# Fused sharp attention and softplus MLP: softplus halves split back to back, next chunk's scales made one quarter earlier

## Chip, cores and metric

The kernel runs on one core of a Trainium2 chip. The metric is device time in microseconds of one execution, inputs and output in device memory. A profile of one execution is at hand; its engines are PE (matmul; PEld is its weight load), DVE (VectorE), ACT (ScalarE), POOL (GpSimd) and SP, which issues DMAs.

## Reference

Attention keeps only scores within `tau` of the row's maximum, and its output goes through a two-layer MLP with softplus.

```python
scores = scale * q @ k.T                       # 8 batches, 8 heads, 576 rows, head size 64
thresh = max(scores, -1) - tau                 # tau = 0.02
scores = where(scores >= thresh, scores, -1e9)
attn = exp(scores - max); attn = attn / (sum(attn) + 1e-9)
x = (attn @ v) -> [4608, 512]                  # heads side by side
h = x @ w_in                                   # [4608, 2048]
out = (max(h, 0) + log1p(exp(-|h|))) @ w_out   # [4608, 512]
```

The inputs q, k, v and w_in are drawn some six times as large as the setup functions alone would give.

## The kernel before

**Attention.** A unit is one batch and two heads: 32 units of nine tiles of 128 query rows, 288 tiles in all. For each tile PE writes the scores `s` (line 480) into one of two PSUM banks; DVE takes the negated row maximum (`negm`); ACT makes `e_all` by the exponential and then the threshold `thr`; DVE masks `e_all` in place, reading the scores again, and only then is that bank free for the scores two tiles on. POOL writes the upper 16-bit half of the masked weights into `h` (the function `weights_hi`), DVE writes the remainder beside it (`weights_lo`, the DVE rows `h<-e_all,h`), a DMA transposes both, and PE multiplies them by v (`pv`, line 591). ACT copies and DVE adds the two parts of `pv` into `xp`.

**MLP.** Tokens go through the MLP in ten chunks: eight of 512 tokens, one for each batch, and two of 256 with the last 64 rows of four batches. For a chunk, `hidden` makes 16 slices of the hidden layer (line 712), each of 12 matmuls, since x and w_in are kept as two 16-bit halves. ACT takes softplus of two slices at a time and scales them (`st`). `parts_of` then splits one slice into its two 16-bit halves on POOL: a TENSOR_SCALAR for the upper half and a TENSOR_TENSOR for the lower one, named `g` in the profile. `project` multiplies by w_out (line 776); a quarter is four slices, and its results are added in SBUF (`acc`) by DVE. In the last quarter of a chunk the products of slices 12 and 13 come first, and the splits of slices 14 and 15 are held in `waits` until those products of the quarter's first output tile have been written into the program; the products with slices 14 and 15 end that output tile.

**Scales.** Before a chunk, `x_scale` makes the scale of x, and `split_x` scales and splits its four columns of `xp` into `xh` and `xl` (ACT, then POOL). `h_scales` makes three small tiles of 128x4 (three DVE instructions, in the profile `c<-p_i,sx` and two `c<-c`), which the softplus needs, and `o_scales` a fourth (`c<-c,p_o`), which `acc` needs. In the chunks after the first they are made when the chunk's first `hidden` and its first `project` are written.

**Order of the work.** The attention tiles lead. For each tile the string `PAT` says in which order its steps and slices of MLP work are written. `defer(n, f)` runs `f` at the n-th `point()` from now, and there are two points in a tile. From tile `TQ` on, the classes `Queue` keep DVE, ACT and POOL in exactly the order written; PE's order and that of the DMAs are set by the scheduler. `prep` is the list of the 32 pieces of weight conversion still to be written; two tiles pass from one piece to the next, so it runs empty at about tile 62 of 288, in the first chunk.

Of the kernel before, what the change touches and what calls it, by code (L numbers as in the profile page):

```python
# [65 lines left out]
def tile_kernel(ctx: ExitStack, tc: tile.TileContext, q, k, v, tau, w_in, w_out, out):  # L66
# [108 lines left out]
    def inverse(out_, p):  # L175

        vec.tensor_scalar(out=out_.bitcast(U32), in0=p.bitcast(U32), scalar1=EXP, scalar2=None, op0=ALU.bitwise_xor)

    def halves(hi, lo, x):
        pool.tensor_scalar(out=hi, in0=x, scalar1=1.0, scalar2=1.0, op0=ALU.mult, op1=ALU.mult)  # L180
        pool.tensor_tensor(out=lo, in0=x, in1=hi, op=ALU.subtract)
# [70 lines left out]
    def need(*key):  # L252

        while key not in ready:
            if prep and not later:
                _, f, a = prep.pop(0)
                f(*a)
            else:
                force()
# [384 lines left out]
    def load_x(u, cc):  # L644

        if u.main:
            return
        for b in range(QB):
            need("q", NPAIR * (QB * u.b + b) + cc)
        st = fpool.tile([P, QB * SR], F32, tag="xst", name=f"xst_{u.n}_{cc}")  # L650
        u.st[cc] = st
        nc.sync.dma_start(st, x_d[u.b][:, cc, :])

    def x_scale(u):
        n = NPAIR * (1 if u.main else QB)
        for i in range(n):
            need("v", n * u.b + i)

        u.sx, u.px = [cpool.tile([P, 1], F32, tag=f"sx{i}", bufs=2, name=f"sx{i}_{u.n}") for i in range(2)]
        u.ch, u.g_top, u.sg, u.co = [cpool.tile([P, NFC // 4], F32, tag=f"c{i}", bufs=2, name=f"c{i}_{u.n}")  # L660
                                     for i in range(4)]
        vec.tensor_reduce(u.sx, v_scale[:, n * u.b:n * (u.b + 1)], axis=AX.X, op=ALU.min)
        inverse(u.px, u.sx)

    def h_scales(u, g):

        if g in u.scaled:
            return
        c = slice(g, g + 1) if u.n == 0 else slice(0, NFC // 4)
        u.scaled |= set(range(c.start, c.stop))  # L670
        vec.tensor_scalar(out=u.ch[:, c], in0=p_w["i"][:, c], scalar1=u.px, scalar2=0.25, op0=ALU.mult, op1=ALU.mult)
        vec.tensor_scalar(out=u.g_top[:, c], in0=u.ch[:, c], scalar1=2.0 ** 26, scalar2=2.0 ** -13,
                          op0=ALU.mult, op1=ALU.max)
        inverse(u.sg[:, c], u.g_top[:, c])

    def o_scales(u, g):

        if g in u.unscaled:
            return
        c = slice(g, g + 1) if u.n == 0 else slice(0, NFC // 4)  # L680
        u.unscaled |= set(range(c.start, c.stop))
        vec.scalar_tensor_tensor(out=u.co[:, c], in0=u.g_top[:, c], scalar=0.25, in1=p_w["o"][:, c],
                                 op0=ALU.mult, op1=ALU.mult)

    def split_x(u, cc, n=0):
        per = 2 * TC // u.T
        if cc % per == 0:
            for l, tag in ((u.h, "xh"), (u.l, "xl")):
                t = fpool.tile([P, 2 * TC], F16, tag=tag, name=f"{tag}_{u.n}_{cc}")
                l += [t[:, i * u.T:(i + 1) * u.T] for i in range(per)]  # L690
        if u.main:
            need("x", NPAIR * u.b + cc)
            st = units[NPAIR * u.b + cc].xp[:, 0:SM]
        else:
            st = u.st.pop(cc)
        act.activation(st, st, AF.Copy, scale=u.sx)
        defer(n, lambda: halves(u.h[cc], u.l[cc], st))
# [23 lines left out]
    def softplus(u, full):  # L721


        ts, last_ = [], None
        with tc.high_priority(SPP):
            for fc, bank in reversed(full):
                t = fpool.tile([P, TC], F32, tag="st", bufs=NST, name=f"st_{u.n}_{fc}")
                i = act.activation(t, bank, AF.Softplus, scale=u.ch[:, fc // 4:fc // 4 + 1]).ins
                if last_ is not None:
                    tc.add_manual_dep(i, last_.name, mybir.DependencyInfo(  # L730
                        mybir.DependencyClass.NoSync, mybir.DependencyReason.DATA), reason="one table load")
                last_ = i
                ts.append((fc, t))
            for fc, t in reversed(ts):
                act.activation(t, t, AF.Copy, scale=u.sg[:, fc // 4:fc // 4 + 1])
        def parts():
            if u.n in waits:
                waits[u.n].append(parts)
                return
            for n, (fc, t) in enumerate(reversed(ts)):  # L740
                defer(n, lambda fc=fc, t=t: parts_of(u, fc, t))
        defer(HD[1], parts)

    waits = {}
# [2 lines left out]
    def parts_of(u, fc, t):  # L747

        home, tags, bufs = (fpool, ("gh", "gl"), NG)
        if u.tail:  # L750
            spare = [("kT", "kT", 2), ("qT0", "qT1", 1), ("nat", "nat", 2), ("vt", "vt", 2)]
            i = later_g[0] % (NG + len(spare))
            later_g[0] += 1
            if i >= NG:
                *tags, bufs = spare[i - NG]
                home = apool
        gh, gl = [home.tile([P, TC], F16, tag=tags[i], bufs=bufs, name=f"g{i}_{u.n}_{fc}") for i in range(2)]
        halves(gh, gl, t)
        for i in range(TC // u.T):
            c = slice(i * u.T, (i + 1) * u.T)  # L760
            u.g[fc + i] = (gh[:, c], gl[:, c])
# [49 lines left out]
    nq = NFC // QF  # L811
# [3 lines left out]
    def order():  # L815
        out_, at_ = [], 0
        for u in chunks:
            both = u.tail and u.n + 1 < len(chunks)
            for qt in range(nq):
                end = NFC * (u.n + (2 if both and qt == nq - 1 else 1))  # L820
                to = min(end, NFC * u.n + QF * (qt + 1) + (LT if u.tail else LS if u.T < TC else NG - QF))
                first_ = [("h", i // NFC, i % NFC) for i in range(at_, to)]
                at_ = max(at_, to)
                if qt == nq - 1 and not u.tail and u.T == TC:


                    last_o = out_.pop()[:4]
                    early.add(last_o[1:])
                    out_ += [("w", u.n), *first_, (*last_o, 0)]
                else:  # L830
                    out_ += first_

                x = u.n + 1 < len(chunks) and qt == nq - (2 if u.tail else 1)
                from_ = 1 if ("o", u.n, nq - 2, u.T // P - 1)[1:] in early and not u.tail else 0
                out_ += [("o", u.n, qt, tb, from_ + tb if x else -1) for tb in range(u.T // P)]
        return out_

    def stream():
        for cc in range(len(X0), NCC):
            split_x(chunks[0], cc)  # L840
        for it in order():
            u = chunks[it[1]]
            if it[0] == "h":
                yield from hidden(u, it[2])
                continue
            if it[0] == "w":
                waits[u.n] = []
                continue
            if it[4] >= 0:

                nx = chunks[u.n + 1]
                per = NCC * P // u.T
                for cc in range(max(0, (it[4] - 1) * per), min(NCC, it[4] * per)):
                    split_x(nx, cc)
                    if cc + 2 < NCC:
                        load_x(nx, cc + 2)
                if it[4] == 0:
                    x_scale(nx)
                    load_x(nx, 0)
                    load_x(nx, 1)  # L860
            yield from project(u, it[2], it[3])
            if it[4] >= 0 and it[3] == u.T // P - 1 and (u.n, it[2], it[3]) not in early:
                for cc in range(it[4] * per, NCC):
                    split_x(nx, cc)
# [6 lines left out]
    def defer(n, f):  # L871
        if n == 0:
            f()
        else:
            later.append((now["p"] + n, f))
# [8 lines left out]
    def force():  # L884
        _, f = later.pop(0)
        f()
# [8 lines left out]
    for n, (main, b, from_) in enumerate(spans):  # L895
        u = Chunk()
# [4 lines left out]
        u.tail = from_ >= NS  # L901
        chunks.append(u)
    ffn = stream()

    def target(g):
# [7 lines left out]
    prep = []  # L913
    for kind, g in WL:
        for m in range(4):
            n = len(prep)
# [167 lines left out]
```

## Time and profile before

| | |
|---|---|
| median of 3 runs | 1319.87 us (1319.84 to 1323.7) |
| the profiled execution | 1319.59 us, of which the instructions span 1317.8 us |
| busy, share of the span | PE 95%, DVE 71%, POOL 70%, ACT 69% |
| granted PE clock, mean | 0.994 |

The profile's page gives for each engine its busy time, for groups of instructions the count, the busy time and the idle time of the engine just ahead of them, and names what ended that idle time. A row of the timeline gives the start and length of one piece of work, and in brackets how long its engine had been idle and what released it. Matmuls overlap, so a PE with no idle time may still lose some time between two starts.

### The profile page before, as it was taken

The numbers are of one execution on the slowest core, as the hardware profiler recorded it, in microseconds if no ns is written. First come the engines' busy times: TensorE is split into PE (matmuls) and PEld (weight loads), VectorE is DVE, ScalarE is ACT, GpSimd is POOL, SyncE is SP. The second block draws the span as 40 slices with busy tenths as digits, with TensorE's granted clock in tenths as the row PEclk, the third lists the DMA queues.
The fourth block names the chain that finished last, engine by engine and source line by source line (L and its number), as shares of the span: only waits on it lengthen the run. The fifth ranks groups of instructions, "written<-read, shape, count | busy, mean of one in ns | idle before, by whom it ended". The sixth has DMA issues, their size and how long they took to land.

```text
span 1317.8 us, 21688 instructions
## 1 busy us (share of the span) xinstructions
PE 1245.7 (95%) x7153; PEld 752.0 (57%) x7153; DVE 936.2 (71%) x1738; ACT 907.2 (69%) x1715; POOL 920.2 (70%) x987
## 2 busy tenths in 40 slices
PE   5988988899999999998999899999999999999998
PEld 4655544455566566665666566655656755554455
DVE  5878888988878787888787877886677666640011
ACT  5877887886877677776777697768675867643321
POOL 2577788888777777778877786787666787564333
PEclk9999999999999999999999999999999999999999
DMA  4544458867876678787877787776667665530010
GB/s 127 159 139 126 125 129 165 180 112 149 160 149 146 139 161 152 150 148 161 149 143 145 161 149 142 145 150 132 130 125 163 115 132 114 98 78 17 1 40 17
DMA packets 395521, 168.79 MB, mean 128 GB/s; under 512 B 350448, under 2 KB 376464, under 8 KB 395408
## 3 DMA queue, kind: packets, MB, share of 16 engines
q1 hardware_dynamic: 395408, 167.40, 61.6%
q8 instruction: 57, 0.93, 0.3%
q14 instruction: 56, 0.46, 0.1%
HBM read 56.62 MB, written 10.63 MB: 51 GB/s over the span
## 4 chain that ended last, share of the span: by engine, by line
PE 57%; ACT 15%; POOL 12%; DVE 8%; issue 6%; DMA 2%; SPq 0%; POOLq 0%; ACTq 0%; DVEq 0%
PE o L776 20%; PE h L712 17%; PE s L480 9%; PE pv L591 6%; ACT L156 4%; ACT st L156 4%; POOL g L156 2%; ACT e_all L156 2%; DVE negm L156 2%; PE pv L550 2%; DVE e_all L156 2%; POOL xl L156 2%; PE tr L420 2%; POOL h L156 1%; POOL w_i L156 1%
## 5 line engine op out<-in xcount | busy, mean ns | idle before, releaser
L776 PE MATMUL o<-w_o,g 128*128 128x512 f16 x1728 | 407.9, 382 | 13.9 <-POOL g L156 11.0
L712 PE MATMUL h<-xh,w_i 128*128 128x512 f16 (+1 forms) x1280 | 360.7, 358 | 3.6 <-ACT kT L156 1.9
L156 POOL TENSOR_SCALAR h<-e_all 128x576 f16<-128x576 f32 x243 | 239.3, 985 | 121.5 <-DVE e_all L156 114.9
L156 ACT ACTIVATE e_all<-s,negm 128x576 f32<-128x576 f32 x288 | 213.8, 742 | 132.3 <-DVE negm L156 129.8
L712 PEld LDWEIGHTS <-w_i 128*128 128x128 f16 x1920 | 179.4, 98 | 165.9 <-issue 7.4
L776 PEld LDWEIGHTS <-g 128*128 128x128 f16 x1728 | 159.1, 98 | 191.4 <-POOL g L156 16.3
L156 DVE SCALAR_TENSOR_TENSOR e_all<-s,thr,e_all 128x576 f32<-128x576 f32 x288 | 233.0, 809 | 49.3 <-ACT thr L156 48.8
L156 DVE TENSOR_REDUCE negm<-s 128x1 f32<-128x576 f32 x288 | 215.2, 747 | 73.2 <-PE s L480 72.1
L156 DVE SCALAR_TENSOR_TENSOR h<-e_all,h 128x576 f16<-128x576 f32 x243 | 237.7, 978 | 2.5 <-POOL h L156 2.5
L712 PE MATMUL h<-xl,w_i 128*128 128x512 f16 (+1 forms) x640 | 229.4, 358 | 0.5 <-POOL xl L156 0.5
L156 POOL TENSOR_SCALAR g<-st 128x512 f16<-128x512 f32 x144 | 99.5, 691 | 165.1 <-ACT st L156 156.9
L156 DVE SCALAR_TENSOR_TENSOR acc<-o,c,acc 128x512 f32<-128x512 f32 x108 | 80.2, 743 | 171.8 <-PE o L776 110.6
L156 POOL TENSOR_TENSOR g<-st,g 128x512 f16<-128x512 f32 x144 | 171.2, 1189 | 12.0
L480 PE MATMUL s<-kT,q 128*128 128x288 f32 x768 | 152.9, 328 | 16.1 <-DVE e_all L156 13.6
L156 ACT ACT_TABLE_LOAD x119 | 152.7, 1283 | 3.9 <-DVE negm L156 1.9
L591 PE MATMUL pv<-eT,vt 128*128 128x288 f16 x1080 | 153.6, 288 | 1.2 <-DVE xp L156 0.4
L156 ACT ACTIVATE st<-h,c 128x512 f32<-128x512 f32 x144 | 91.2, 684 | 76.2 <-PE h L712 75.4
L480 PEld LDWEIGHTS s<-kT,q 128*128 128x128 f32 x768 | 115.0, 192 | 49.1 <-DVE e_all L156 35.6
L591 PEld LDWEIGHTS <-vt 128*128 128x128 f16 x1080 | 99.9, 98 | 37.9 <-issue 2.0
L480 PE MATMUL s<-kT,qT 128*128 128x288 f32 x512 | 107.3, 331 | 10.5 <-DVE e_all L156 8.7
L156 ACT COPY xp<-pv 64x288 f32<-64x288 f32 (+3 forms) x133 | 50.7, 385 | 87.1 <-PE pv L591 82.9
L156 ACT ACTIVATE st<-st,c 128x512 f32<-128x512 f32 x144 | 96.3, 716 | 2.3
(113 smaller groups left out, 1512.7 us busy)
## 6 DMA issues: line engine op xcount, KB each, us to landing
q<-q SPq DMA_DIRECT2D x62, 192.0 KB
kn<-in_k_dram SPq DMA_DIRECT2D x32, 256.0 KB
qn<-in_q_dram SPq DMA_DIRECT2D x32, 256.0 KB
vn<-in_v_dram SPq DMA_DIRECT2D x32, 256.0 KB
wc_i<-in_moe_w_in_dram SPq DMA_DIRECT2D x16, 512.0 KB
wc_o<-in_moe_w_out_dram SPq DMA_DIRECT2D x16, 512.0 KB
qT<-qT SPq DMA_DIRECT2D x62, 128.0 KB
out_dram<-acc SPq DMA_DIRECT2D x14, 512.0 KB
```

The costliest lines, as they stand in the source:

```text
L156: i = getattr(self.eng, name)(*args, **kwargs)
L420: nc.tensor.transpose(pr[:, c * P:(c + 1) * P], src, identr)
L480: nc.tensor.matmul(sp[:, hf, 0:HS], lhs, s.kT[j][:, hf * HS:(hf + 1) * HS], start=(m == 0), stop=(m == len(parts) - 1))
L550: nc.tensor.matmul(o[0:D, 0:n], s.vn[k_, 5 * j + c, :], h[k_, c, 0:n], start=(c == 0), stop=(c == NC))
L591: nc.tensor.matmul(o[:, 0:HS], s.vt[:, 5 * j + c, :], s.eT[j][:, c + i, x0:x0 + HS], start=(c == 0 and i == 0), stop=(c == NC and i > 0))
L712: nc.tensor.matmul(bank[:, i * u.T:(i + 1) * u.T], wi[g, cc][:, a, e], x[cc], start=(cc == 0 and m == 0), stop=(cc == NCC - 1 and m == 2))
L776: nc.tensor.matmul(o, u.g[fc][m // 2][:, sl], wo[fc][:, m % 2, :], start=(n == 0), stop=(n == 3 * QF - 1))
```

## The change

Two places of the program are touched. In `softplus`, the two slices of a pair were split at one point and the next. While `prep` still holds weight conversions this stays; after that both are split at the same point, one behind the other. In `stream`, right behind `x_scale` for the next chunk (written ahead of the last output tile of the running chunk's third quarter, and in the chunks of 256 tokens and the last ones at the start of a late quarter), the four small scale instructions for the next chunk are written at once; `need` makes sure that the scales of all weight blocks exist there. The later calls of `h_scales` and `o_scales` then find them made.

```diff
             for n, (fc, t) in enumerate(reversed(ts)):
-                defer(n, lambda fc=fc, t=t: parts_of(u, fc, t))
+                defer(n if prep else 0, lambda fc=fc, t=t: parts_of(u, fc, t))
         defer(HD[1], parts)
...
                 if it[4] == 0:
                     x_scale(nx)
+                    need("i", nq - 1)
+                    need("o", nq - 1)
+                    h_scales(nx, 0)
+                    o_scales(nx, 0)
                     load_x(nx, 0)
                     load_x(nx, 1)
```

On POOL, at the end of chunk 1, the pair of slices 14 and 15 (`g_1_14`, `g_1_15`) stands as follows before; `xh` and `xl` are the first columns of x for chunk 2:

```order
L156 TENSOR_SCALAR g_1_14_5206<-st_14_5173 128x512
L156 TENSOR_TENSOR g_1_14_5207<-st_14_5173,g_1_14_5206 128x512
L156 TENSOR_SCALAR h_132<-e_all 128x576
L156 TENSOR_SCALAR xh_0_5226<-xp_3783 128x512
L156 TENSOR_TENSOR xl_0_5227<-xp_3783,xh_0_5226 128x512
L156 TENSOR_SCALAR g_1_15_5233<-st_15_5171 128x512
L156 TENSOR_TENSOR g_1_15_5234<-st_15_5171,g_1_15_5233 128x512
L156 TENSOR_SCALAR h_132<-e_all 128x576
```

and in the changed kernel:

```order
L156 TENSOR_SCALAR g_1_14_5210<-st_14_5177 128x512
L156 TENSOR_TENSOR g_1_14_5211<-st_14_5177,g_1_14_5210 128x512
L156 TENSOR_SCALAR g_1_15_5214<-st_15_5175 128x512
L156 TENSOR_TENSOR g_1_15_5215<-st_15_5175,g_1_15_5214 128x512
L156 TENSOR_SCALAR h_132<-e_all 128x576
L156 TENSOR_SCALAR xh_0_5234<-xp_3787 128x512
L156 TENSOR_TENSOR xl_0_5235<-xp_3787,xh_0_5234 128x512
```

Slice 15 has moved ahead of one `h` and of the first `xh` and `xl`. Within a chunk the same happens to every pair, as on POOL for slices 4 and 5 of chunk 2, before:

```order
L156 TENSOR_SCALAR g_2_4_5768<-st_4_5747 128x512
L156 TENSOR_TENSOR g_2_4_5769<-st_4_5747,g_2_4_5768 128x512
L156 TENSOR_SCALAR h_132<-e_all 128x576
L156 TENSOR_SCALAR g_2_5_5789<-st_5_5745 128x512
L156 TENSOR_TENSOR g_2_5_5790<-st_5_5745,g_2_5_5789 128x512
L156 TENSOR_SCALAR h_132<-e_all 128x576
```

and in the changed kernel:

```order
L156 TENSOR_SCALAR g_2_4_5768<-st_4_5748 128x512
L156 TENSOR_TENSOR g_2_4_5769<-st_4_5748,g_2_4_5768 128x512
L156 TENSOR_SCALAR g_2_5_5772<-st_5_5746 128x512
L156 TENSOR_TENSOR g_2_5_5773<-st_5_5746,g_2_5_5772 128x512
L156 TENSOR_SCALAR h_132<-e_all 128x576 x2
```

The first of the two `h` now stands behind two more instructions and right in front of the second. The third place is DVE at the start of chunk 2, where the scales stood before, between the remainder of one tile's weights and the addition into `xp`:

```order
L156 SCALAR_TENSOR_TENSOR h_132<-e_all,h_132 128x576
L156 TENSOR_SCALAR c_2_5158<-p_i,sx_2_5157 128x4
L156 TENSOR_SCALAR c_2_5159<-c_2_5158 128x4
L156 TENSOR_SCALAR c_2_5160<-c_2_5159 128x4
L156 TENSOR_TENSOR xp_5415<-pv_0_5416,xp_5415 64x288
```

and where they stand in the changed kernel, on DVE in chunk 1, between the scale of x for chunk 2 and the row maximum of a tile:

```order
L156 TENSOR_SCALAR sx_2_5157<-sx_2_5156 128x1
L156 TENSOR_SCALAR c_2_5158<-p_i,sx_2_5157 128x4
L156 TENSOR_SCALAR c_2_5159<-c_2_5158 128x4
L156 TENSOR_SCALAR c_2_5160<-c_2_5159 128x4
L156 SCALAR_TENSOR_TENSOR c_2_5161<-c_2_5159,p_o 128x4
L156 TENSOR_REDUCE negm_5_5220<-s_131 128x1
```

The first three moved by some 28 rows and the fourth, which stood in chunk 2 ahead of a row maximum, by some 60. ACT's order is the same in both kernels. On PE single products change places at the ends of chunk 0 and chunk 5, and on SP a few DMAs.

## The prediction

> **What bounds the kernel now.** I read the page first (busy shares), then the stretches by stage, then PE's waits grouped by releaser, then the timeline around the longest of them.
>
> ```profile
> PE 1245.7 (95%) x7153; PEld 752.0 (57%) x7153; DVE 936.2 (71%) x1738; ACT 907.2 (69%) x1715; POOL 920.2 (70%) x987
> ...
> 595.50:733.70 138.20, 134.45 (x793) 82.39 (x794) 110.77 (x202) 100.94 (x185) 104.46 (x112) 1.00 0.77 149
> ```
>
> PE is busy for 134.45 of 138.20 us in chunk 3, at full clock, while DVE has 110.77 and POOL 104.46. So what counts is idle time of PE, and what is late for PE. PE's waits that the change can touch, of those grouped by releaser (us in total, times, longest):
>
> ```profile
> PE s L480 <- DVE e_all L156: 22.4, 27, 3.7
> PE o L776 <- POOL g L156: 11.0, 12, 1.9
> PE tr L413 <- DVE xp L156: 4.3, 6, 1.2
> ```
>
> The second is what the first edit is about, the third what the second edit is about, and the first is where both can do harm.
>
> **First edit, at the chunk's end.** POOL, then PE, in the end of chunk 1:
>
> ```profile
> 450.14 1.16 POOL L156 TENSOR_TENSOR g<-st,g 128x512 f16<-128x512 f32 x1
> 451.27 0.67 POOL L156 TENSOR_SCALAR h<-e_all 128x576 f16<-128x576 f32 x1
> 453.92 0.62 POOL L156 TENSOR_SCALAR xh<-xp 128x512 f16<-128x512 f32 x1 [1.98 <-ACT xp L156]
> 454.63 1.53 POOL L156 TENSOR_TENSOR xl<-xp,xh 128x512 f16<-128x512 f32 x1
> 456.13 0.61 POOL L156 TENSOR_SCALAR g<-st 128x512 f16<-128x512 f32 x1
> 456.83 1.15 POOL L156 TENSOR_TENSOR g<-st,g 128x512 f16<-128x512 f32 x1
> ...
> 453.20 1.69 PE L776 MATMUL o<-w_o,g 128*128 128x512 f16 x7
> 456.80 0.82 PE L776 MATMUL o<-w_o,g 128*128 128x512 f16 x3 [1.92 <-POOL g L156]
> 458.04 1.03 PE L776 MATMUL o<-w_o,g 128*128 128x512 f16 x2 [0.42 <-POOL g L156]
> ...
> 454.00 1.14 DVE L156 SCALAR_TENSOR_TENSOR h<-e_all,h 128x576 f16<-128x576 f32 x1
> 458.68 0.75 DVE L156 SCALAR_TENSOR_TENSOR acc<-o,c,acc 128x512 f32<-128x512 f32 x1 [3.04 <-PE o L776]
> ```
>
> The half of slice 14 is done at 451.30. Slice 15 then waits behind h, behind 1.98 us in which POOL is idle for x, and behind xh and xl, until 456.13. PE has used everything else by 454.89 (453.20 + 1.69) and idles 1.92 + 0.42 = 2.34 us. With slice 15 directly behind slice 14 its halves are done at about 451.30 + 0.62 + 0.08 + 1.15 = 453.1, before PE asks. The h that it pushes back ends at 453.8, still ahead of 454.00, where DVE reads it, and of xh at 453.92: POOL's idle time pays. So the whole 2.34 goes, and over all chunk ends the row's 11.0 us. What is late next: DVE waits 3.04 us there for the same PE product, so it moves forward with PE; I see no other wait within the 2.3 us. Ends for this term: 11.0, and half of it if x, scores or a bank take over.
>
> **First edit, within a chunk.** Here no PE wait on g is to be won, and h comes later by the 0.62 + 0.08 + 1.16 of one split. Slices 4 and 5 of chunk 2, POOL, DVE, PE:
>
> ```profile
> 501.39 1.16 POOL L156 TENSOR_TENSOR g<-st,g 128x512 f16<-128x512 f32 x1
> 502.52 0.67 POOL L156 TENSOR_SCALAR h<-e_all 128x576 f16<-128x576 f32 x1
> 503.86 1.16 POOL L156 TENSOR_TENSOR g<-st,g 128x512 f16<-128x512 f32 x1
> 504.98 1.18 POOL L156 TENSOR_SCALAR h<-e_all 128x576 f16<-128x576 f32 x1
> ...
> 503.63 0.82 DVE L156 SCALAR_TENSOR_TENSOR e_all<-s,thr,e_all 128x576 f32<-128x576 f32 x1 [1.80 <-ACT thr L156]
> 504.37 1.26 DVE L156 SCALAR_TENSOR_TENSOR h<-e_all,h 128x576 f16<-128x576 f32 x1
> 505.55 0.74 DVE L156 TENSOR_REDUCE negm<-s 128x1 f32<-128x576 f32 x1
> 506.22 0.80 DVE L156 SCALAR_TENSOR_TENSOR e_all<-s,thr,e_all 128x576 f32<-128x576 f32 x1
> ...
> 507.09 0.79 PE L480 MATMUL s<-kT,q 128*128 128x288 f32 x4
> ```
>
> The reader is to see two things. PE's scores start at 507.09, 0.07 us behind the end of DVE's mask at 507.02: any delay of DVE here is a delay of PE. And DVE's remainder at 504.37 takes 1.26 us, of which the first part passes until POOL's TENSOR_TENSOR ends at 505.02; POOL's next h, begun at 504.98, takes 1.18 instead of 0.67, until DVE is through. These two instructions don't run side by side; the second to come waits. In the changed order h ends at about 502.52 + 1.86 + 0.67 = 505.05, the next h is next on POOL and runs until 505.7, and DVE's remainder, which can't start before 505.1, ends at 505.7 + 0.62 = 6.3, that is 506.3 instead of 505.63. DVE and the scores behind it: 0.65 us late. If DVE got in ahead of the second h it would be some 0.2 us late.
>
> On this the Trainium skill ("SBUF — State Buffer", section on who interferes with whom) says that a VectorE instruction with two SBUF inputs and a GpSimd one that reads SBUF share a port pair as an exclusive lock, and that the order of issue decides who waits. The rows above agree (1.26 and 1.18 us). The rule speaks against this edit: by it the second h wins and the place costs the larger of my two values; without it the place would cost the smaller.
>
> Other pairs of the chunk, POOL's h between the two slices and the DVE row that reads it: slices 0 and 1, then 2 and 3, then 8 and 9:
>
> ```profile
> 485.58 0.67 POOL L156 TENSOR_SCALAR h<-e_all 128x576 f16<-128x576 f32 x1
> ...
> 487.21 1.49 DVE L156 SCALAR_TENSOR_TENSOR h<-e_all,h 128x576 f16<-128x576 f32 x1
> 488.73 0.46 DVE L156 TENSOR_TENSOR xp<-pv,xp 64x288 f32<-64x288 f32 x1
> ...
> 493.92 0.67 POOL L156 TENSOR_SCALAR h<-e_all 128x576 f16<-128x576 f32 x1
> ...
> 496.90 1.32 DVE L156 SCALAR_TENSOR_TENSOR h<-e_all,h 128x576 f16<-128x576 f32 x1
> ...
> 535.58 0.67 POOL L156 TENSOR_SCALAR h<-e_all 128x576 f16<-128x576 f32 x1
> ...
> 537.75 0.94 DVE L156 SCALAR_TENSOR_TENSOR h<-e_all,h 128x576 f16<-128x576 f32 x1
> 540.14 1.88 DVE L156 SCALAR_TENSOR_TENSOR h<-e_all,h 128x576 f16<-128x576 f32 x1
> ```
>
> For 0 and 1 h would be ready at 485.58 + 1.86 + 0.67 = 488.1 and the remainder, behind one more POOL instruction, end at 489.1 instead of 488.70; PE waits for that xp just behind, so I put 0.4. For 8 and 9 the remainder ends some 0.6 later than 538.69, but the next one (1.88 us, most of it waiting for POOL) absorbs part: 0.3, and the same for 12 and 13, which follow the same pattern one unit on. For slices 2 and 3 h would come at 493.92 + 2.53 = 496.45, and DVE asks at 496.90: nothing, and likewise for 6 and 7 and for 10 and 11, where DVE asks later still. Sum for a chunk 0.65 + 0.4 + 0.3 + 0.3 = 1.65, for the four chunks 1 to 4 about 6.6 us. Behind chunk 4 DVE has time, as this stretch of chunk 6 and what follows shows, so I cost it at nothing; the cover is DVE's 62.7 idle us there (181.40 - 118.73), and if it failed the price would be that of one more chunk, 1.65.
>
> ```profile
> 998.60:1180.00 181.40, 178.62 (x1099) 112.27 (x1100) 118.73 (x221) 123.53 (x213) 124.08 (x134) 1.00 0.59 115
> ```
>
> Ends for the term: 0, and 0.65 at all seven pairs of four chunks, 28 x 0.65 = 18.2. I stay nearer to the lower end, by the row of slices 2 and 3: three of the seven pairs cost nothing. On SP one load of q's rest rows falls behind two transposes and an output; no wait on it shows. In chunk 0 and chunk 5 PE's products with slice 15 move ahead of scores, as the scheduler now expects them earlier; they are counted in the 11.0.
>
> **Second edit.** No instruction is added; four per chunk move. The start of chunk 4, DVE and PE, then the place to which they go, at the end of chunk 1:
>
> ```profile
> 749.93 0.63 DVE L156 TENSOR_SCALAR c<-p_i,sx 128x4 f32<-128x4 f32 x1
> 750.60 0.38 DVE L156 TENSOR_SCALAR c<-c 128x4 f32<-128x4 f32 x2
> 750.88 0.44 DVE L156 TENSOR_TENSOR xp<-pv,xp 64x288 f32<-64x288 f32 x1
> ...
> 751.38 0.28 PE L413 MATMUL tr<-identr,k 128*128 128x128 f32 x1 [1.08 <-DVE xp L156]
> ...
> 447.25 0.76 DVE L156 TENSOR_REDUCE negm<-s 128x1 f32<-128x576 f32 x1 [0.60 <-PE s L480]
> 450.41 0.46 DVE L156 TENSOR_TENSOR xp<-pv,xp 64x288 f32<-64x288 f32 x1 [1.00 <-ACT xp L156]
> ```
>
> Without them xp starts 0.95 us earlier (750.88 - 749.93), and PE's 1.08 shrinks to about 0.1. Over the six waits of the group, 4.3 us, I take 4.0. At the new place they cost DVE their 0.63 + 0.38 + about 0.2, of which 0.60 is idle time before negm and the rest lies ahead of another idle time of 1.00: nothing reaches PE. If that cover fails, 0.6 at each of nine chunks, 5.4. Ends: -4.3 and +1.1.
>
> **The sum.** -11.0 + 6.6 - 4.0 = -8.4 us on the profiled 1319.59 gives 1311.2. The median of the runs, 1319.87, lies 0.28 above it: I forecast 1311.5, 0.6% faster. About 0.3%, 4 us, is what a measurement can tell from no change here.
>
> **Rivals.** (1) The delays of h cost nothing, because DVE gets in between the two h or makes it up at its next wait: 1319.9 - 15.0 = 1304.9, and some 1306 if a little stays. For it speaks that DVE is idle for 27 of 138 us in a chunk; against it 0.07 us between mask and scores. (2) The wait at the chunk's end is only replaced (by x, by scores, by a bank), half of 11.0 stays, and the delays of h come in full: 1319.9 - 5.5 - 4.0 + 6.6 = 1317. With the second edit failing too, 1321. Against it: no other engine is late within those 2.3 us. (3) Slower: the h behind two splits. Every moved pair of the chunks 1 to 4 makes DVE's mask late, by the lock above, as the worst does. At 28 x 0.65 = 18.2 the gain of 15.0 is gone (1323.1); it decides from 0.54 us a pair on. Seven pairs a chunk would have to behave like slices 4 and 5; three don't ask for h in time to notice. By the lock rule of the Trainium skill alone, at every pair, one would come to this case.
>
> **Chances.** As forecast, 1307 to 1315: 0.5. Rival 1: 0.22. Rival 2: 0.18, most of it within 0.3%. Rival 3: 0.1, mostly slower. So faster by over 0.3% 0.74, within 0.3% 0.18, slower 0.08. The range takes in most of rival 1 and most of rival 2: 1305 to 1319.
>
> **What would show it.** Right: PE's waits of o for POOL's g fall from 11.0 to under 1 us, those of tr for xp at line 413 from 4.3 to under 1; PE's waits of s for e_all or DVE's waits for POOL's h (2.5 us before) grow by a few us; chunks 1 to 4 shorten from 138.2 to about 136.6 us each, the part from 1180 on keeps its length. Wrong: the waits on g stay, or a chunk is no shorter though they went, or the gain is 15 us and h's delay appears nowhere.

## The result and the profile after

The changed kernel takes 1306.32 us (median of 4 runs, 1305.69 to 1307.61) against 1319.86 us (4 runs) of the kernel before: ratio 0.9892, 95% interval 0.9872 to 0.9912; between the medians lie 13.5 us. A second series (e5 below) gave 0.9906 (0.9891 to 0.9922). The forecast was 1311.5 us in a range of 1305 to 1319. The sign and the range held; the gain is 1.6 times the forecast 8.4 us. The profiled execution took 1307.61 us, its instructions span 1305.5 us.

The busy times on the page of the changed kernel:

```profile
PE 1238.5 (95%) x7153; PEld 750.8 (58%) x7153; DVE 930.4 (71%) x1738; ACT 906.0 (69%) x1715; POOL 913.2 (70%) x987
```

PE's work is the same, 7153 matmuls, and so are DVE's and POOL's counts. PE's waits of the changed kernel, grouped by releaser (us in total, times, longest):

```profile
PE s L480 <- DVE e_all L156: 26.6, 29, 4.1
...
PE topv L378 <- DVE xp L156: 1.5, 2, 1.0
PE pv L591 <- DVE xp L156: 1.4, 3, 0.5
```

Both waits that the edits were about have left the list: of o for POOL's g (11.0 before) and of tr at line 413 for DVE's xp (4.3 before) no row of 0.3 us or more is left. In their place stand 4.2 us more of s behind DVE's mask (22.4 before), the two small groups behind xp, and a few single waits of up to 1.0 us. So 15.3 us of waits went, and the largest of what came is 4.2.

Where in the program the time went is seen in stretches of 36 tiles, cut at the ends of DVE's masks of tiles 143, 179, 215, 251 and 287, with the tail behind them; first the kernel before, then the changed one (length, then busy time of PE, PEld, DVE, ACT, POOL with counts, PE clock, DMA share, GB/s):

```profile
571.50:709.70 138.20, 134.50 (x793) 82.41 (x792) 110.83 (x205) 100.94 (x185) 104.51 (x113) 1.00 0.78 149
709.70:847.90 138.20, 134.49 (x793) 82.34 (x792) 110.83 (x203) 100.89 (x185) 104.60 (x113) 1.00 0.76 149
847.90:1003.00 155.10, 151.13 (x874) 90.58 (x873) 112.84 (x210) 107.89 (x195) 113.16 (x123) 1.00 0.68 134
1003.00:1164.90 161.90, 159.12 (x989) 101.65 (x989) 110.67 (x204) 114.37 (x198) 113.52 (x120) 1.00 0.61 120
1164.90:1317.80 152.90, 147.80 (x792) 77.19 (x789) 23.63 (x44) 45.31 (x72) 59.44 (x70) 1.00 0.10 27
```

```profile
569.50:704.30 134.80, 133.72 (x793) 82.69 (x792) 109.61 (x204) 100.76 (x185) 102.95 (x113) 1.00 0.80 153
704.30:839.00 134.70, 133.65 (x793) 82.59 (x792) 109.56 (x204) 100.74 (x185) 102.89 (x113) 1.00 0.80 153
839.00:990.50 151.50, 150.49 (x874) 90.78 (x873) 112.76 (x216) 107.18 (x193) 111.91 (x122) 1.00 0.67 137
990.50:1152.50 162.00, 159.35 (x990) 101.36 (x989) 106.85 (x201) 115.29 (x199) 113.26 (x122) 1.00 0.63 120
1152.50:1305.50 153.00, 147.89 (x793) 77.28 (x790) 23.13 (x44) 45.25 (x72) 59.31 (x70) 1.00 0.10 28
```

A chunk in steady state is 3.4 to 3.6 us shorter, where the forecast had 1.6. The last stretch has kept its length, as forecast, and so has the one ahead of it. Two earlier ones belong to the sum: tiles 107 to 143 are 4.0 us shorter (some 0.6 us of it is a drop of PE's clock in the kernel before, see e3 and e4), and tiles 71 to 107 (the end of chunk 0 and the start of chunk 1), 138.81 us before, take 139.12: there the edits brought nothing in sum; why is told further down.

The end of chunk 1 in the changed kernel, POOL, PE and DVE (the whole is 2.0 us later here than in the kernel before: the mask of tile 107 ends at 434.78 us against 432.79):

```profile
451.38 0.62 POOL L156 TENSOR_SCALAR g<-st 128x512 f16<-128x512 f32 x1 [1.13 <-PE o L776]
452.08 1.54 POOL L156 TENSOR_TENSOR g<-st,g 128x512 f16<-128x512 f32 x1
453.59 0.61 POOL L156 TENSOR_SCALAR g<-st 128x512 f16<-128x512 f32 x1
454.29 1.16 POOL L156 TENSOR_TENSOR g<-st,g 128x512 f16<-128x512 f32 x1
455.42 0.67 POOL L156 TENSOR_SCALAR h<-e_all 128x576 f16<-128x576 f32 x1
...
455.14 2.76 PE L776 MATMUL o<-w_o,g 128*128 128x512 f16 x12
457.74 0.38 PE L378 MATMUL topv<-identr,vtop 128*128 128x128 f32 x2
...
456.12 1.15 DVE L156 SCALAR_TENSOR_TENSOR h<-e_all,h 128x576 f16<-128x576 f32 x1
```

The twelve products that ran as 7, 3 and 2 with two waits between now run in one piece of 2.76 us; slice 15's halves are done at 455.45, before PE comes to the products that read them. The h that was pushed back ends at 456.09 and DVE's remainder takes it at 456.12, with no idle time in its row. Counted from the end of slice 14's split (453.62), slice 15 is done 1.83 us and the h 2.47 us later, where the prediction had 1.85 and 2.52: that part came out as it drew it.

### The profile page after: what moved, and what is told of

The parts are those of the page before. It is cut to its first block, busy times and chain, and to the rows that moved or that the text cites. A ratio compares the mean times of both kernels' runs of the same rounds, so it can differ in the third digit from the quotient of the medians.

```text
span 1305.5 us, 21701 instructions
## 1 busy us (share of the span) xinstructions
PE 1238.5 (95%) x7153; PEld 750.8 (58%) x7153; DVE 930.4 (71%) x1738; ACT 906.0 (69%) x1715; POOL 913.2 (70%) x987
## 4 chain that ended last, share of the span: by engine, by line
PE 45%; ACT 18%; POOL 13%; DVE 12%; issue 7%; DMA 3%; SPq 1%; POOLq 0%; DVEq 0%; ACTq 0%
PE o L776 15%; PE h L712 14%; PE s L480 7%; ACT st L156 6%; ACT L156 5%; PE pv L591 5%; POOL g L156 4%; DVE e_all L156 3%; DVE negm L156 3%; ACT e_all L156 3%; DVE h L156 2%; PE pv L550 2%; POOL h L156 2%; POOL w_i L156 1%; POOL xl L156 1%
## 5 line engine op out<-in xcount | busy, mean ns | idle before, releaser
L776 PE MATMUL o<-w_o,g 128*128 128x512 f16 x1728 | 402.7, 380 | 3.1 <-DVE xp L156 1.6
L156 POOL TENSOR_SCALAR h<-e_all 128x576 f16<-128x576 f32 x243 | 228.0, 941 | 114.3 <-DVE e_all L156 108.3
L156 DVE SCALAR_TENSOR_TENSOR h<-e_all,h 128x576 f16<-128x576 f32 x243 | 235.8, 971 | 19.6 <-POOL h L156 19.2
L480 PE MATMUL s<-kT,q 128*128 128x288 f32 x768 | 153.1, 328 | 22.4 <-DVE e_all L156 18.5
```

The source lines that it names most:

```text
L156: i = getattr(self.eng, name)(*args, **kwargs)
L480: nc.tensor.matmul(sp[:, hf, 0:HS], lhs, s.kT[j][:, hf * HS:(hf + 1) * HS], start=(m == 0), stop=(m == len(parts) - 1))
L776: nc.tensor.matmul(o, u.g[fc][m // 2][:, sl], wo[fc][:, m % 2, :], start=(n == 0), stop=(n == 3 * QF - 1))
```

## The experiments

The softplus line and the scales were varied one by one. All ratios are to runs of the kernel before on the same chip. "End pair" means slices 14 and 15 of a chunk, "inner pairs" the seven others.

| run | end pair | inner pairs | scales | median us | ratio (95%) |
|---|---|---|---|---|---|
| e1_scales_only | apart | apart | early | 1315.79 | 0.9954 (0.9941 to 0.9968) |
| e3_end_pair_and_scales | apart (edit without effect) | apart | early | 1317.45 | 0.9969 (0.9957 to 0.9981) |
| e2_splits_only | together | together | late | 1313.91 | 0.9953 (0.9934 to 0.9971) |
| e4_inner_pairs_only | together (edit without effect) | together | late | 1315.61 | 0.9958 (0.9943 to 0.9973) |
| e5_after_again | together | together | early | 1307.82 | 0.9906 (0.9891 to 0.9922) |
| e6_end_pair_and_scales | together | apart | early | 1302.88 | 0.9866 (0.9851 to 0.9881) |
| e7_inner_pairs_only | apart | together | late | 1326.77 | 1.0046 (1.0033 to 1.006) |
| e8_h_first | together | one point on | early | 1305.46 | 0.9882 (0.9866 to 0.9898) |
| e9_end_pair_alone | together | apart | late | 1309.24 | 0.9917 (0.9899 to 0.9935) |
| e10_end_pair_three_scales | together | apart | early, three of four | 1300.81 | 0.9844 (0.9825 to 0.9864) |

**e1: the scales alone.** The softplus line stays as before; the four lines for the scales are in.

```diff
                     x_scale(nx)
+                    need("i", nq - 1)
+                    need("o", nq - 1)
+                    h_scales(nx, 0)
+                    o_scales(nx, 0)
```

> Only the second edit (the four small scale instructions moved one quarter ahead); pairs are split as before. Theory 'three parts' (end-of-chunk pair, pairs within a chunk, scales each have their own price, which add): the changed kernel's 13.5 us holds about 6 us of this part, since the start-to-start loss of PE at the starts of chunks 1 to 5 was 1.3, 0.3, 1.3, 1.2 and 0.8 us, and about 0.3 more goes where the fourth instruction stood: 1313 to 1315.5 us. Rival 'one part': nearly all comes from the end-of-chunk pair, and DVE only waits elsewhere instead: 1318 to 1320.

Measured 1315.79 us, about 5.7 us under the kernel before, more than the 4.0 of the prediction. The waits of tr at line 413 for xp are gone; those of o for POOL's g stay with 9.3 us in 8 waits.

**e2: the splits alone.** The softplus line of the change, without the scales.

```diff
-                defer(n, lambda fc=fc, t=t: parts_of(u, fc, t))
+                defer(n if prep else 0, lambda fc=fc, t=t: parts_of(u, fc, t))
```

> Only the first edit (both slices of a pair split back to back after the weight conversion); scales as before. 'Three parts': end of chunk 2.65 us start to start in each of four chunks won, about 1.6 us a chunk lost to the later h: 1313 to 1316 us, and together with the scales-only run the two gains add to 12 to 15 us. 'One part': 1307 to 1309.

Measured 1313.91 us. The row to look at among PE's waits of e2 is the one of the chunk's start, 4.3 us in 6 waits before:

```profile
PE tr L413 <- DVE xp L156: 8.3, 6, 1.8
```

With nothing to wait for at the chunk's end, PE reaches the next chunk's start earlier and waits longer there for xp. So 4 us of the first edit's gain are given back some 17 us on, unless the second edit takes that wait away.

**e3 and e4: an end pair by a flag, a miss.** A flag was set where the splits of slices 14 and 15 are put into `waits`, and the split distance was to depend on it: for e3 as shown, with the scales; for e4 `n if prep or held else 0`, without them.

```diff
+        held = []
...
+                held.append(1)
                 waits[u.n].append(parts)
...
-                defer(n, lambda fc=fc, t=t: parts_of(u, fc, t))
+                defer(0 if held else n, lambda fc=fc, t=t: parts_of(u, fc, t))
```

> Only the held pair (slices 14 and 15) is split back to back; the pairs within a chunk stay one point apart; scales moved. 'Three parts': the price of the later h (some 1.6 us in each of four chunks, more in chunk 0) is not paid: 5 to 8 us below the changed kernel's 1306.3, that is 1298 to 1301; DVE's waits for POOL's h fall from 19.2 us back to some 2.5. Rival 'free h' (rival 1 of the prediction: the later h costs nothing on PE): 1305 to 1307.

> Only the pairs within a chunk are split back to back; the held pair stays apart and the scales stay late. 'Three parts': nothing is won, the later h is paid: 5 to 8 us slower than before, 1325 to 1328 us. 'Free h': 1319 to 1321.

Neither expectation could be tried. The condition never holds: softplus defers its splits by some points, and by then the quarter's first products have been written. So what stands above, that the splits of slices 14 and 15 are held in `waits`, does not happen in this program. All engines of e3 have the instructions of e1 in e1's order, and those of e4 the order of e2. The two runs are therefore repeats: 1317.45 beside 1315.79 and 1315.61 beside 1313.91, so the same program differs by 1.7 us between two medians on one chip. Smaller differences are not read from medians below. The profiles show where it lies: until the end of tile 71 two executions of one program differ by up to 4.9 us (e1 and e3), behind it their stretches of 36 tiles agree to 0.1 us, but for two between e1 and e3 (1.4 and 1.6 us, of opposite sign).

The granted clock of PE in the traces accounts for these differences. Between 25 and 140 us it stands at half for 7 us in e1 and for 17 us in e3. In the two later stretches it falls to half for 3.4 us, once in each run: from 730.6 us on in e1 and from 872.7 us on in e3, both times at the two waits on g (1.9 and 0.4 us) of a chunk's end. The kernel before has such a drop at the end of chunk 1, from 457.7 us on; the row has the clock, 0.56 on the mean of this window, as its third number from the end:

```profile
458.00:461.50 3.50, 3.46 (x12) 2.23 (x13) 2.36 (x6) 0.15 (x1) 3.33 (x5) 0.56 0.62 142
```

Between tile 71 and the tail, all four profiles in which the end pair is split apart have such drops (before, e1 and e3 one each, e7 two), each 0.9 to 1.7 us behind the end of the longer wait, and none of the eight profiles with the end pair back to back has one. So the first edit also takes away these drops, which the prediction didn't have. By the starts of the same instructions in two runs, one drop costs PE about 1.5 us. In the kernel before 0.6 of them are left in the stretch (138.74 us for tiles 107 to 143 against 138.15 for the next 36), since PE, being late, then waits only 0.17 us for xp at the start of chunk 2, where it waits 1.10 at that of chunk 3.

**e5: the change again**, beside e6 to e8.

> The changed kernel unaltered, as the yardstick on this chip for the runs beside it: 13.5 us below before by both theories, 1306 to 1309 us.

Measured 1307.82 us, 0.9906: the result repeats.

**e6: end pair and scales, inner pairs as before.** The pair is now told by its slice number.

```diff
-                defer(n, lambda fc=fc, t=t: parts_of(u, fc, t))
+                defer(0 if ts[0][0] >= NFC - 2 else n, lambda fc=fc, t=t: parts_of(u, fc, t))
```

> Of the pairs only that of slices 14 and 15 is split back to back, told by its slice number; the pairs within a chunk stay one point apart; scales moved. 'Later h has its price' (0.4 to 0.6 us of PE at each of four places in each of the chunks 1 to 4, some 2 us in chunk 0): 5 to 9 us below the changed kernel, DVE's waits for POOL's h back at some 2.5 us. 'Later h is free': the same as the changed kernel within 1.5 us.

Measured 1302.88 us, 4.9 us under the changed kernel in the same series. The inner pairs cost time, as the prediction held. How is seen in DVE's group of remainders, first in the changed kernel, then in e6 (busy, mean ns | idle time ahead, and what ended it):

```profile
L156 DVE SCALAR_TENSOR_TENSOR h<-e_all,h 128x576 f16<-128x576 f32 x243 | 235.8, 971 | 19.6 <-POOL h L156 19.2
```

```profile
L156 DVE SCALAR_TENSOR_TENSOR h<-e_all,h 128x576 f16<-128x576 f32 x243 | 235.8, 971 | 4.9 <-POOL h L156 4.3
```

DVE waits 19.2 us for POOL's h in the changed kernel, 4.3 in e6 and 2.5 in the kernel before.

**e7: the inner pairs alone**, end pair apart, scales late.

```diff
-                defer(n, lambda fc=fc, t=t: parts_of(u, fc, t))
+                defer(n if prep or ts[0][0] >= NFC - 2 else 0, lambda fc=fc, t=t: parts_of(u, fc, t))
```

> Only the pairs within a chunk are split back to back; slices 14 and 15 stay one point apart; scales as before. 'Later h has its price': 5 to 9 us slower than before, PE's waits of o for POOL's g near 11 us again. 'Later h is free': as before within 2 us.

Measured 1326.77 us, 0.46% slower (interval 0.33 to 0.6%), 5.9 us. This part of the change by itself makes the kernel slower.

**e8: inner pairs one point on**, so that POOL's h stands ahead of both splits of a pair: as e6, with `n if prep else 0 if ts[0][0] >= NFC - 2 else 1` as the distance.

> Scales moved, slices 14 and 15 back to back; the pairs within a chunk are back to back too, but at the later of the two points, so that h goes ahead of both. 'Later h has its price': like e6 or up to 2 us faster, since DVE finds h done; if PE asks for these slices soon, waits of o for POOL's g come in and it is slower. 'Later h is free': as the changed kernel within 1.5 us.

Measured 1305.46 us, between e5 (1307.82) and e6. DVE's waits for POOL's h are 6.9 us instead of 19.5. In a steady chunk, moving h ahead heals all that e5 loses against e6 (134.16 us for tiles 143 to 179, and 134.13 in e6). Over the whole program it heals about half: tiles 71 to 107 take 0.8 us and tiles 251 to 287 1.5 us longer than in e6, with one wait of 1.40 us for xp (0.28 in e6) and one of 0.64 us for POOL's g. Nothing is won over leaving the inner pairs alone.

**e9: the end pair alone**, e6 without the scales.

> Only slices 14 and 15 are split back to back; pairs within a chunk one point apart; scales as before. By difference (e2 minus e7) the end pair is worth some 12 us of PE in the records from the end of chunk 0 on: 1307 to 1310 us. If part of it turns into a longer wait of PE's tr at line 413 for DVE's xp at the chunk's start, that group grows from 4.3 to some 8 us and moving the scales on top is then worth 6 to 8 us (to e6). If the two edits simply add, the group stays at 4.3 and the scales are worth the 5.5 us of e1.

Measured 1309.24 us. Its start of chunk 3 shows the interaction, DVE and then PE:

```profile
603.28 1.36 DVE L156 TENSOR_SCALAR c<-p_i,sx 128x4 f32<-128x4 f32 x1
604.67 0.81 DVE L156 TENSOR_SCALAR c<-c 128x4 f32<-128x4 f32 x2
605.39 0.44 DVE L156 TENSOR_TENSOR xp<-pv,xp 64x288 f32<-64x288 f32 x1
...
605.89 0.28 PE L413 MATMUL tr<-identr,k 128*128 128x128 f32 x1 [1.68 <-DVE xp L156]
```

PE's wait is 1.68 us, where the kernel before has 1.10 at the start of the same chunk (613.24 us): the three small scale instructions, ahead of xp, now hold up a PE that is there earlier. One of them takes 1.36 us.

**e10: three of the four scales**, e6 without the line `o_scales(nx, 0)`.

> Like e6, but the fourth scale instruction (c<-c,p_o) stays in the next chunk, ahead of a row maximum. Idle rows show nothing there, start to start PE lost 0.33 us a chunk: 1 to 2 us slower than e6 by the start-to-start reading, equal to e6 by the idle-row reading. With medians known to about 1.5 us the profile's stretch from chunk 1 on decides.

Measured 1300.81 us, the fastest of all: 1.6% under the kernel before (interval 1.4 to 1.8%). The expectation, that it would be a little slower than e6, was wrong: the 0.3 us that PE loses ahead of some scores in e6, which I had laid to the fourth scale, are there in e10 too. A chunk in steady state is equally long in both. They differ by 1.7 us between tiles 71 and 107, and by 0.6 and 0.3 us in the stretches from tile 215 and from tile 251 on. At the end of chunk 0 the profiles show why. In e6 DVE has there

```profile
314.49 0.83 DVE L156 SCALAR_TENSOR_TENSOR c<-c,p_o 128x4 f32<-128x4 f32 x1
...
318.72 0.46 DVE L156 TENSOR_TENSOR xp<-pv,xp 64x288 f32<-64x288 f32 x1
```

and PE waits 0.42 us for `acc` and 0.96 us for xp. In e10 the first row is missing, xp starts 1.3 us earlier relative to PE's work, and of both waits of PE 0.14 us is left. So at that place the fourth scale is better left in the next chunk. By the medians, 1302.88 and 1300.81 us on two chips with overlapping intervals of the ratios, it stays open how much e10 is better than e6.

## Why the prediction was right, and where it was off

**The terms in a steady chunk.** The 36 tiles between the ends of DVE's masks of tiles 143 and 179, in the kernel before, then with scales alone (e3), end pair alone (e9), both (e6), inner pairs alone (e7), and in the changed kernel; length first:

```profile
571.45:709.60 138.15, 134.45 (x794) 82.41 (x792) 110.78 (x203) 100.89 (x185) 104.46 (x113) 1.00 0.78 149
```

```profile
572.89:709.90 137.01, 134.30 (x794) 82.40 (x792) 111.40 (x205) 100.75 (x185) 104.59 (x113) 1.00 0.77 151
```

```profile
566.19:702.18 135.99, 134.04 (x794) 82.48 (x792) 110.20 (x203) 100.75 (x185) 104.16 (x113) 1.00 0.79 152
```

```profile
569.52:703.65 134.13, 133.85 (x794) 82.61 (x792) 110.04 (x205) 100.85 (x185) 104.88 (x113) 1.00 0.80 154
```

```profile
575.71:714.52 138.81, 134.21 (x794) 82.35 (x792) 110.39 (x204) 100.85 (x185) 103.03 (x113) 1.00 0.76 149
```

```profile
569.43:704.23 134.80, 133.72 (x794) 82.69 (x792) 109.61 (x203) 100.76 (x185) 102.95 (x113) 1.00 0.80 153
```

| term, per steady chunk | forecast us | measured us |
|---|---|---|
| scales alone | about -1.0 | -1.14 |
| end pair alone | -2.34 | -2.16 |
| end pair and scales | -3.3 | -4.02 |
| inner pairs | +1.65 | +0.66 alone, +0.67 on top of e6 |
| all | -1.7 | -3.35 |

Of the 1.7 us between the last row's two numbers, 1.0 is the cost of the inner pairs and 0.7 the pair of terms at the chunk's boundary.

**The chunk's boundary: right in mechanism, mis-sized in sum.** The end wait goes as a whole, the scales' wait too, and the two add up to more than the terms by themselves, since each term was read from a trace in which the other wait still stood: the end pair alone gives back 0.6 us at the start (1.68 against 1.10), which the scales then return. The prediction named as late next at the end only DVE, and did not follow PE on to the chunk's start. Besides, idle rows leave out a part of each loss. The end pair alone takes 2.34 us of idle time away at the end and adds 0.6 at the start, 1.74 net; the chunk shortens by 2.16. Of that difference, about 0.17 for each of the two waits that went is in the matmul rows themselves: one product takes 0.38 in its row and a second one adds only 0.21, so some 0.17 us ahead of each wait is shown as busy though nothing could start. By the starts of the same products in the kernel before and in e9 the two waits cost 2.07 and 0.58 us, where their idle rows have 1.91 and 0.42.

**The inner pairs: the mechanism came out to the hundredth at its place; the net price did not.** Slices 4 and 5 of chunk 2 in the changed kernel, POOL, DVE and PE:

```profile
500.46 1.16 POOL L156 TENSOR_TENSOR g<-st,g 128x512 f16<-128x512 f32 x1
501.58 1.30 POOL L156 TENSOR_SCALAR h<-e_all 128x576 f16<-128x576 f32 x2
...
502.29 1.21 DVE L156 SCALAR_TENSOR_TENSOR h<-e_all,h 128x576 f16<-128x576 f32 x1 [0.48 <-POOL h L156]
503.42 0.75 DVE L156 TENSOR_REDUCE negm<-s 128x1 f32<-128x576 f32 x1
504.08 0.80 DVE L156 SCALAR_TENSOR_TENSOR e_all<-s,thr,e_all 128x576 f32<-128x576 f32 x1
504.82 0.08 DVE L156 DVE_READ_ACCUMULATOR e_all<-s,thr,e_all 128x1 f32 x1
...
504.95 0.79 PE L480 MATMUL s<-kT,q 128*128 128x288 f32 x4 [0.35 <-DVE e_all L156]
```

The first h ends 0.67 us after 501.58, at 502.25; the second follows at once, DVE's remainder starts behind the first and takes 1.21 us (0.74 is the shortest of all its rows), because it gets through only when the second h is done at 502.88: it ends at 503.50, 0.62 us behind that and 1.25 us behind the first h, and the prediction had 506.3 - 505.05 = 1.25. That is also what the Trainium skill ("SBUF — State Buffer", section "Who interferes with whom") makes of it, an exclusive lock in order of issue, and the trace agrees. PE waits 0.35 us for the mask behind it. But losses within a chunk don't add up. The same tiles of chunk 3, PE's rows in the changed kernel, then in the one before:

```profile
621.82 0.90 PE L591 MATMUL pv<-eT,vt 128*128 128x288 f16 x6 [0.48 <-DVE xp L156]
...
639.71 0.80 PE L480 MATMUL s<-kT,q 128*128 128x288 f32 x4 [0.34 <-DVE e_all L156]
```

```profile
635.24 0.80 PE L480 MATMUL s<-kT,qT 128*128 128x288 f32 x4 [0.17 <-DVE e_all L156]
```

The changed kernel has the losses at slices 0 and 1 and at slices 4 and 5, as forecast, but the kernel before has one between them (0.17 idle) which is gone: a PE that has just been held up by 0.48 us no longer comes too early to the next mask. At slices 8 and 9 and at 12 and 13 PE's waits are only 0.14 and 0.12. Idle rows alone don't add up to the net; the starts of the same instructions in the changed kernel and in e6 do. At slices 0 and 1 PE falls 0.41 us behind e6 and makes up 0.39 at the next mask, for which e6 waits and the changed kernel doesn't; at slices 8 and 9 and at 12 and 13 it falls 0.49 and 0.47 us behind and has made that up within two tiles; only at slices 4 and 5 does it fall 0.69 us behind (0.65 was forecast) and stay there. So the net is 0.67 us a chunk, not 1.65: one of the four prices is paid for good.

**Why the sum for the inner pairs still was close.** Over the whole program they cost 5.9 us by the medians of e7 and 4.9 by e5 against e6; 6.6 was forecast. That is luck in part. Tiles 107 to 215, as long as three of the four chunks to which the forecast put it all, hold only about a third of it (2.2 us in e7, 1.8 between e6 and the changed kernel), and 2.4 us fall between tiles 71 and 107 (141.17 us in e7 against 138.81 before; 139.12 against 136.77 in e6), a stretch whose end of chunk 0 was costed at nothing. There the rows of the changed kernel are

```profile
298.25 1.39 PE L591 MATMUL pv<-eT,vt 128*128 128x288 f16 x10 [0.81 <-ACT qT L156]
...
318.67 0.53 PE L420 MATMUL tr<-identr,q 128*128 128x128 f32 x4 [0.42 <-DVE acc L156]
...
322.76 0.49 PE L378 MATMUL topv<-identr,vtop 128*128 128x128 f32 x2 [0.96 <-DVE xp L156]
```

The first is a wait that the kernel before and e6 lack there and e7 has; with the waits that follow it PE falls 1.7 us behind e6 between tiles 72 and 75. The other two are at the end of chunk 0, in e6 as well. They come with the scales: e1, where the end pair is apart, has waits of 0.42 and 0.69 us at the same two places, e9 (late scales) and e10 (no fourth scale there) have at most 0.14. So at this chunk's end the second edit puts waits in the place of those on g that the first takes away. These two losses are why tiles 71 to 107 became no shorter: without them, in e10, they take 135.09 us.

**The rivals.** (1), the delays of h for nothing, named 1304.9 us, which is near the result, but its mechanism is disproved by e6 and e7: the delays cost 5 to 6 us. Half of its reasoning is true all the same, since three of the four delays of a steady chunk are made up soon after. (2), the end wait only replaced, holds in part while the scales are late: of its 11.0 us some 4 come back as waits for xp at the chunks' starts (e2 and e9, 8.3 us against 4.3). With the scales early nothing of that is left, and the two waits at the end of chunk 0 come from the scales. (3), every pair as dear as the worst, is out: 0.67 us for the seven of a chunk, not 0.65 for each.

**The failed step** is the sum's size, in the boundary term and in the price per chunk of the inner pairs: -11.0 - 4.0 = -15.0 was forecast for end pair and scales, and e6 measures -18.0 by its medians (1320.89 - 1302.88). The -8.4 has a boundary term 3 us too small, and a cost term 0.7 to 1.7 us too large. One statement of the second edit failed as well: that nothing of it reaches PE at the new place is true in the steady chunks and false at the end of chunk 0, where it costs 1.4 us. DVE's waits for POOL's h were to grow by a few us and grew by 16.7; most of that lies where DVE had time, so that it says little on PE.

## What to carry to other kernels

When a wait of the bounding engine is taken away, follow that engine to its next waits before writing the gain down: there the wait comes back or another edit becomes worth more, so two edits at one boundary are priced together. Delays of a supplier are not to be added up along a stretch either, since an engine that was just held up is no longer early for the next wait. And an edit that applies to eight pairs is worth splitting into the one that gains and the seven that pay: here the end pair with the scales, inner pairs as before, beats both kernels (e6, e10).

## What the runs showed of the hardware

A DVE instruction of 128x4 elements that takes 0.27 us in one place takes 1.36 us at the start of chunk 3 in e9, while POOL's TENSOR_TENSOR on vt runs (602.83 to 604.61; at 1.78 us it is itself longer than the 1.40 that most of its kind take). The two rows, of the changed kernel and of POOL in e9:

```profile
448.64 0.27 DVE L156 TENSOR_SCALAR c<-p_i,sx 128x4 f32<-128x4 f32 x1
```

```profile
602.83 1.78 POOL L156 TENSOR_TENSOR vt<-vn,vt 128x640 f16<-128x640 f32 x1
```

The small one ends at 604.64, right behind POOL's, and the one of 0.27 us ends 0.02 us behind an h of POOL as well. In the twelve profiles this instruction starts 89 times while POOL runs another, and each time it ends 0.02 or 0.03 us behind that one; the 19 times that POOL runs nothing it takes 0.22 or 0.23 us. So this tiny instruction pays the whole remaining length of a large one on the other engine, and where it stands decides what it costs. Row maximum and mask of DVE, which read PSUM, keep 0.74 to 0.76 and 0.80 to 0.82 us in all rows shown here.

PE's granted clock fell to half for 3.4 us behind waits as short as 1.9 and 0.4 us at a chunk's end, at one or two chunk ends of an execution and not at the others with the same waits. What decides at which, no run here shows.
